# Streaming the key and value caches in 8 MB units through three slots, with the K transpose in place, instead of 4 MB units through five

## Chip, cores, metric

One core of one Trainium2 chip. The metric is the device time of one execution in microseconds. The kernel before takes 662.42 us (median of 4 runs, 661.61 to 662.64). Most differences here are well under 1%, so nearly all kernels are measured in five rounds, with each kernel run beside the kernel before on the same chip.

## The reference

One decode step: layer norm, attention of 16 query heads over 8 cached K/V heads of 32,768 tokens, output projection, then layer norm and a small feed-forward net with the mish activation.

```python
def _A_ref(x, k_cache, v_cache, wq, wo):        # x [1,1,448], caches [1,8,32768,256] bf16
    q = (x @ wq).reshape(B, Sq, 16, 256).transpose(0, 2, 1, 3)
    k = jnp.repeat(k_cache, 2, axis=1); v = jnp.repeat(v_cache, 2, axis=1)
    p = softmax(einsum("bhqd,bhkd->bhqk", q, k) * 256 ** -0.5)
    o = einsum("bhqk,bhkd->bhqd", p, v)
    return o.transpose(0, 2, 1, 3).reshape(B, Sq, 4096) @ wo
h  = x + _A_ref(layernorm(x), ...)
h2 = h + mish(layernorm(h) @ w1 + b1) @ w2      # w1 [448,1792], w2 [1792,448]
```

The two caches are 268 MB, nearly all the bytes that are read.

## The kernel before

A unit is TU = 64 tokens per partition: 128 x 64 tokens x 256 values of bf16, 4 MB, one DMA. Each partition reads one contiguous row of 64 x 512 B = 32 KB. Units go into a ring of five slots.

```python
TU = 64; CT = 16                       # tokens per partition in a unit, in a group
RING = 5 * TU * Dh * 2                 # bytes per partition

def pump():                            # issue loads, in order, as long as there is room
    while st["next"] < len(loads):
        key, nbytes, issue = loads[st["next"]]
        ...                            # next place in the ring
        if any(a < pos + nbytes and pos < b for a, b, _ in live):
            return
        ...
        tiles[key] = issue(pos)

def kv_issue(src, g, u, a, b):
    def issue(pos):
        t = region(pos, (b - a) * Dh).rearrange("p (t d) -> p t d", d=Dh)
        rows = src[0, g, u * UT:(u + 1) * UT, :].rearrange("(p t) d -> p t d", p=P)
        nc.sync.dma_start(out=t, in_=rows[:, a:b, :])
        return t
    return issue
```

K is transposed in blocks of 32 x 32 by VectorE (DVE) into one of three small tiles; the unit's slot is then free for the next load. TensorE (PE) does 8 matmuls for each group of 16 tokens.

```python
def transpose_next():                  # one group ahead of the matmuls
    nc.vector.transpose(out=kt_ring[n % 3][:]..., in_=tiles[key][:, t0:t0 + CT]...)
    if t0 + CT == key[3] - key[2]:
        done(key)                      # K slot free
```

K runs one head ahead of V (NU = 4 units). The softmax of a head is cut into small steps (`i0` to `i4`: VectorE, PE and ScalarE in turn) which `hook()` puts between the groups that follow. At the end, `wo` (the output projection, 3.7 MB) is loaded after the last K unit, ahead of the last four V units, and the projections of the first seven heads stand ahead of the third-last and second-last V unit. Behind the last V unit come w1 and w2.

Of the kernel before, what the change touches and what calls it, by code (L numbers as in the profile page):

```python
# [24 lines left out]
def kernel(  # L25
# [13 lines left out]
    nc = tc.nc  # L39
# [5 lines left out]
    F = B_w1.shape[1]  # L45
    assert Dh == 256 and Hq == 2 * G and G == 8 and HD == 4096 and D == 448
    CT = 16
    TU = 64
    UT = TU * P
    CPU_ = TU // CT  # L50
    NU = Sk // UT
# [12 lines left out]

    W = 160
    DQ = D // 4
    RING = 5 * TU * Dh * 2

    const = ctx.enter_context(tc.tile_pool(name="const", bufs=1))
    small = ctx.enter_context(tc.tile_pool(name="small", bufs=4))  # L70
    ps = ctx.enter_context(tc.tile_pool(name="ps", bufs=1, space=bass.MemoryType.PSUM))
    ps_m = ctx.enter_context(tc.tile_pool(name="ps_m", bufs=2, space=bass.MemoryType.PSUM))
    ctx.enter_context(tc.manual_schedule())
# [5 lines left out]

    loads = []  # L80
    live = []
    st = {"next": 0, "pos": 0}

    def plan(key, nbytes, issue):
        loads.append((key, nbytes, issue))

    tiles = {}

    def pump():
        while st["next"] < len(loads):  # L90
            key, nbytes, issue = loads[st["next"]]
            pos = st["pos"]
            for _ in range(2):
                if pos + nbytes > RING:
                    pos = 0
                for a, b, kk in live:
                    if kk[0] == "wo" and a < pos + nbytes and pos < b:
                        pos = b
            if any(a < pos + nbytes and pos < b for a, b, _ in live):
                return  # L100
            live.append((pos, pos + nbytes, key))
            tiles[key] = issue(pos)
            st["pos"] = pos + nbytes
            st["next"] += 1

    def done(key):
        live[:] = [x for x in live if x[2] != key]
        pump()
# [45 lines left out]
    NK = G * NU  # L154
    H = TU // 2
    kpieces = {k: [(0, TU)] for k in range(NK)}
    kpieces[0] = [(0, H), (H, TU)]
    vpieces = {v: [(0, TU)] for v in range(NK)}
    vpieces[NK - 2] = [(0, H), (H, TU)]
    vpieces[NK - 1] = [(0, H), (H, H + 16), (H + 16, H + 24), (H + 24, TU)]  # L160
    order = []
    for k in range(NK + NU):
        if k < NK:
            order += [("k", k, a, b) for a, b in kpieces[k]]
        if k >= NU:
            order += [("v", k - NU, a, b) for a, b in vpieces[k - NU]]
        if k == NK - 1:
            order.append(("wo",))
    for kt in range(KTD):
        plan(("wq", kt), HD * 2 if kt < 3 else HD, wq_issue(kt))  # L170
    for key in order:
        if key[0] == "wo":
            plan(key, Hq * 2 * D * 2, wo_issue)
        else:
            g, u = divmod(key[1], NU)
            plan(key, (key[3] - key[2]) * Dh * 2,
                 kv_issue(A_k_cache if key[0] == "k" else A_v_cache, g, u, key[2], key[3]))
    plan(("w1", 0), 7 * F, w1_issue)
    plan(("w2", 0), FT * D * 2, w2_issue)

    xr_bf = const.tile([1, D], BF16)
    nc.scalar.dma_start(out=xr_bf[:], in_=A_x[0])
    b1r = big[0:1, RING // 2 - F:RING // 2]
    nc.scalar.dma_start(out=b1r, in_=B_b1.rearrange("(o f) -> o f", o=1))
    pump()

# [19 lines left out]
    maskT = const.tile([P, KTD], F32)  # L206
    nc.vector.memset(maskT[:], 1.0)
    nc.vector.memset(maskT[0:64, 3:4], 0.0)
    par = const.tile([1, 2, P], F32)
    nc.vector.memset(par[:], 0.0)  # L210
    for hh in range(2):
        nc.vector.memset(par[:, hh].rearrange("o (k e) -> o k e", e=2)[:, :, hh:hh + 1], -1.0)  # L212
    maskpar = const.tile([P, 2], F32)
    nc.vector.tensor_reduce(out=maskpar[:], in_=ident_f[:].rearrange("p (k e) -> p e k", e=2), axis=AX.X, op=ALU.add)  # L214
    hb2 = const.tile([P, KTD, 2], BF16)
# [11 lines left out]
    nc.vector.memset(oT_ps[:], 0.0)  # L227
    nc.vector.memset(hT_ps[:], 0.0)

    kt_ring = [const.tile([P, CT, Dh], BF16, name=f"kt{i}") for i in range(3)]  # L230
    p_ring = [const.tile([P, CT * 32], BF16, name=f"p{i}") for i in range(2)]
    pt_ring = [const.tile([P, CT, 32], BF16, name=f"pt{i}") for i in range(2)]
    rden = const.tile([P, G, 2], F32)
    og = const.tile([P, G, 2, 2], BF16)
# [6 lines left out]
    nc.gpsimd.tensor_scalar(out=vpe[:], in0=mv[:, 1:2], scalar1=EPS, scalar2=None, op0=ALU.add)  # L241
    rstd = small.tile([1, 1], F32, tag="ln_rstd")
    nc.gpsimd.tensor_tensor(out=rstd[:], in0=vpe[:], in1=negh[0:1], op=ALU.pow)  # L243
    xn_bf = const.tile([1, D], BF16)
    nc.vector.tensor_scalar(out=xn_bf[:], in0=xr_bf[:], scalar1=mv[:, 0:1], scalar2=rstd[:, 0:1],
                            op0=ALU.subtract, op1=ALU.mult)
    xeo = const.tile([1, 2, P], BF16)
    nc.vector.memset(xeo[:], 0.0)
    for e in range(2):
        nc.vector.tensor_copy(out=xeo[:, e].rearrange("o (r e) -> o r e", e=2)[:, :, e], in_=xn_bf[:, 3 * P:D])  # L250
# [30 lines left out]
    qrow_ps = ps_m.tile([NCH, P], BF16, tag="m")  # L281
    nc.tensor.transpose(out=qrow_ps[:], in_=qT_sb[:], identity=ident_bf[:])

    chunks = [(("k", k, a, b), k * CPU_ + t // CT, t - a) for k in range(NK) for a, b in kpieces[k] for t in range(a, b, CT)]
    tr = {"n": 0}

    def transpose_next():
        n = tr["n"]
        if n >= len(chunks):
            return  # L290
        key, _, t0 = chunks[n]
        tr["n"] += 1
        nc.vector.transpose(out=kt_ring[n % 3][:].rearrange("p t d -> p (t d)").bitcast(F32),  # L293
                            in_=tiles[key][:, t0:t0 + CT].rearrange("p t d -> p (t d)").bitcast(F32))
        if t0 + CT == key[3] - key[2]:
            done(key)

    Qin = const.tile([P, P], BF16)
    for i in range(4):
# [13 lines left out]
            nc.vector.tensor_copy(out=dst, in_=src)  # L313

    weights(0)
    transpose_next()

    def x_of(j, e):
        jhi, jl = j // 2, j % 2
# [10 lines left out]

    def k_chunk(n):
        g, c = divmod(n, NCK)
        transpose_next()
        if c == NCK // 2 and g + 1 < G:
            weights(g + 1)
        ktv = kt_ring[n % 3][:].rearrange("p t (j b e) -> p t j b e", j=4, b=32, e=2)
        s = s_ring[g % 2]
        for i in range(8):
            j, e = i // 2, i % 2
            nc.tensor.matmul(s[:], lhsT=QW[g % 2][:, x_of(j, e), 30 - 2 * c:30 - 2 * c + P], rhs=ktv[:, :, j, :, e],  # L340
                             start=(c == 0 and i == 0), stop=(c == NCK - 1 and i == 7))
        if c == NCK - 1:
            softmax(g)

    def softmax(g):
        s = s_ring[g % 2]
        p_ = p_ring[g % 2]
        pt = pt_ring[g % 2]
        m = small.tile([P, 1], F32, tag="m1", name=f"m1_{g}")
        mT = ps_m.tile([1, P], F32, tag="m", name=f"mT_{g}")  # L350
        m2 = small.tile([1, 2], F32, tag="m2", name=f"m2_{g}")
        nm_ps = ps_m.tile([P, 1], F32, tag="m", name=f"nm_{g}")
        nm = small.tile([P, 1], F32, tag="nm", name=f"nms_{g}")
        L = small.tile([P, 1], F32, tag="L", name=f"L_{g}")
        Lm = small.tile([P, 2], F32, tag="Lm", name=f"Lm_{g}")
        den = ps_m.tile([P, 2], F32, tag="m", name=f"den_{g}")

        def i0():
            nc.vector.reduce_max(out=m[:], in_=s[:], axis=AX.X)  # L359
            nc.tensor.transpose(out=mT[:], in_=m[:], identity=ident_f[:])  # L360

        def i1():
            nc.vector.reduce_max(out=m2[:], in_=mT[:].rearrange("o (k e) -> o e k", e=2), axis=AX.X)  # L363
            for hh in range(2):
                nc.tensor.matmul(nm_ps[:], lhsT=par[:, hh], rhs=m2[:, hh:hh + 1], start=(hh == 0), stop=(hh == 1))  # L365

        def i2():
            nc.vector.tensor_copy(out=nm[:], in_=nm_ps[:])  # L368
            nc.scalar.activation(out=p_[:], in_=s[:], func=ACT.Exp, bias=nm[:], scale=1.0, accum_out=L[:])  # L369

        def i3():
            ready.add(g)
            nc.vector.transpose(out=pt[:].rearrange("p t c -> p (t c)"), in_=p_[:])  # L373
            nc.vector.tensor_scalar(out=Lm[:], in0=maskpar[:], scalar1=L[:, 0:1], scalar2=None, op0=ALU.mult)

        def i4():
            nc.tensor.matmul(den[:], lhsT=ones_f[:], rhs=Lm[:], start=True, stop=True)  # L377
            nc.vector.reciprocal(out=rden[:, g], in_=den[:])  # L378
        pending.extend([lambda: None, i0, i1, i2, i3, i4])

    def v_chunk(g, c, vn, t0):
        assert g in ready
        pt = pt_ring[g % 2]
        o = o_ring[g % 2]
        last = NCK - 1 if g < G - 1 else NCK - 1 - CPU_
        for t2 in range(CT // 2):
            nc.tensor.matmul(o[:], lhsT=pt[:].rearrange("p t c -> p (t c)")[:, 64 * t2 + 2 * c:64 * t2 + 2 * c + 34],  # L387
                             rhs=vn[:, t0 + 2 * t2:t0 + 2 * t2 + 2, :].rearrange("p t d -> p (t d)"),
# [7 lines left out]

    def evac(g):
        o = o_ring[g % 2]
        osb = small.tile([34, 512], F32, tag="osb", bufs=2, name=f"osb_{g}")

        def e0():
            nc.scalar.copy(out=osb[:], in_=o[:])  # L402
# [29 lines left out]
    for key in order:  # L432
# [4 lines left out]
        if kind == "k":  # L437
            for t in range(a, b, CT):
                k_chunk(nk)
                nk += 1  # L440
                hook()
            continue
        if i == NK - 3:
            for gg in range(4 if a == 0 else 0):
                project(gg)
        if i == NK - 2 and a == 0:
            for gg in range(4, G - 1):
                project(gg)
        if i < NK - 1:
            for t in range(a, b, CT):  # L450
                v_chunk(g, u * CPU_ + t // CT, tiles[key], t - a)
                hook()
        else:
            for t in range(a, b, min(CT, b - a)):
                n = min(CT, b - a)
                v_cols(u * CPU_ + t // CT, t % CT, tiles[key][:, t - a:t - a + n], n)
            if pending:
                hook()
        done(key)
    og_copy(G - 1)  # L460
    project(G - 1)
# [108 lines left out]
```

## Time and profile before

| | before |
|---|---|
| time | 662.42 us |
| moved | 279.4 MB, 423 GB/s over the span |
| share of the 16 DMA engines filled by the SyncE queue's packets | 98.9% |
| PE, DVE busy | 78%, 48% |
| one 32 KB packet | 1218 ns (median and mean of 7,808) |
| first engine's landing to the next unit's | 9.713 us for 4 MB, 432 GB/s |

These are lines of the profile's page of the kernel before. The second gives busy time by engine; the DMA row is the mean busy share of the 16 DMA engines in 40 equal slices, in tenths; then packets and the load queue with its share. The last is the costliest group: line, engine, operation, count, then busy us and mean ns, then the engine's idle time before it.

```profile
span 659.8 us, 5982 instructions
PE 516.9 (78%) x2673; PEld 228.1 (35%) x2673; DVE 315.3 (48%) x263; ACT 13.8 (2%) x30; POOL 3.1 (0%) x12
...
DMA  9999999999999999999999999999999999999996
...
DMA packets 14293, 279.37 MB, mean 423 GB/s; under 512 B 1338, under 2 KB 4539, under 8 KB 5308
...
q1 hardware_dynamic: 14264, 278.99, 98.9%
...
L293 DVE STREAM_TRANSPOSE kt<-big 128x2048 f32<-128x2048 f32 x128 | 288.0, 2289 | 217.6 <-DMA big<-in_A_k_cache_dram 191.1
```

The DMA row is full from the first slice to the last but one, while the transposes sit idle for 191 us waiting for K. Loads set the time. Only two things can then shorten it: making the bytes cost less, or making the ends shorter, where the queue has not begun or is already empty.

The end is the second reading. This is PE's timeline of the kernel before: start and length in us, then line, operation, tile and count; in brackets PE's idle time before it and who ended it. The last V unit's direct matmuls are line 427, w1's are L483, w2's L535.

```profile
606.82 0.38 PE L387 MATMUL o<-big,pt 128*34 128x512 bf16 x1
618.53 3.34 PE L387 MATMUL o<-big,pt 128*34 128x512 bf16 x8 [11.34 <-DMA big<-in_A_v_cache_dram]
...
638.51 7.08 PE L387 MATMUL o<-big,pt 128*34 128x512 bf16 x32
645.52 1.75 PE L427 MATMUL oT_ps<-pt,big 128*128 128x2 bf16 x64
...
648.24 1.83 PE L427 MATMUL oT_ps<-pt,big 128*128 128x2 bf16 x64
650.32 0.57 PE L421 MATMUL hT_ps<-og,big 128*128 128x1 bf16 x16 [0.25 <-DVE og L394]
651.14 0.51 PE L483 MATMUL h_ps<-hb,big 128*128 128x2 bf16 x14 [0.26 <-DVE hb L466]
...
655.38 1.48 PE L535 MATMUL y_ps<-big,actT 128*1 128x112 bf16 x56 [1.66 <-DVE actT L520]
```

PE stands idle for 11.3 us while `wo` is loaded ahead of V, and then has no more gap until 650: it is behind its data. The last V piece landed at 647.98 us (all 16 of its completions counted in the trace) and PE finished it only at 650.07.

### The profile page before, as it was taken

To read this page: it belongs to the slowest core of one execution; us is meant where nothing else is said; L and a number is where in the kernel's file an instruction comes from. 1 tells how busy PE (TensorE), PEld (TensorE's weight loads), DVE (VectorE), ACT (ScalarE), POOL (GpSimd) and SP (SyncE) were. 2 spreads that over 40 slices of the span, in tenths; PEclk is the share of its full clock that TensorE was granted. 3 is DMA by queue.
4 is the path that set the end of the run, shared out by engine and by line. 5 is a ranking of instruction groups with operands and counts; after the bars stand their busy time and mean duration, and the time that the engine had idled before them with its cause. 6 is when DMAs were issued, how large, how long until landed. Compare 5 with 4: busy or idle time off the path is not lost.

```text
span 659.8 us, 5982 instructions
## 1 busy us (share of the span) xinstructions
PE 516.9 (78%) x2673; PEld 228.1 (35%) x2673; DVE 315.3 (48%) x263; ACT 13.8 (2%) x30; POOL 3.1 (0%) x12
## 2 busy tenths in 40 slices
PE   3577389949986699748997399974999669978596
PEld 2223134314432244313443144421443224333255
DVE  3599455528345366434654254552744447533001
ACT  1000000000000000000000000000000000000000
POOL 1000000000000000000000000000000000000000
PEclk9989889969998599986999789995999879999696
DMA  9999999999999999999999999999999999999996
GB/s 365 429 444 436 421 438 421 442 421 436 435 422 445 417 440 427 430 433 425 441 421 439 429 430 435 424 435 432 433 428 431 427 436 436 424 433 398 431 414 231
DMA packets 14293, 279.37 MB, mean 423 GB/s; under 512 B 1338, under 2 KB 4539, under 8 KB 5308
## 3 DMA queue, kind: packets, MB, share of 16 engines
q1 hardware_dynamic: 14264, 278.99, 98.9%
q8 instruction: 21, 0.34, 0.2%
q14 instruction: 4, 0.03, 0.0%
q10 hardware_dynamic: 4, 0.00, 0.0%
HBM read 278.99 MB, written 0.00 MB: 423 GB/s over the span
## 4 chain that ended last, share of the span: by engine, by line
issue 98%; DVE 1%; PE 0%; POOL 0%; POOLq 0%; ACT 0%
PE y_ps L535 0%; POOLq L565 0%; DVE stt L237 0%; POOL rstd L243 0%; DVE maskpar L214 0%; DVE par L210 0%; DVE res L538 0%; DVE hq L218 0%; DVE z L506 0%; DVE dn L517 0%; ACT e__3117 L509 0%; POOL vpe L241 0%; DVE dn L516 0%; DVE e L512 0%; DVE par L212 0%
## 5 line engine op out<-in xcount | busy, mean ns | idle before, releaser
L293 DVE STREAM_TRANSPOSE kt<-big 128x2048 f32<-128x2048 f32 x128 | 288.0, 2289 | 217.6 <-DMA big<-in_A_k_cache_dram 191.1
L340 PE MATMUL s<-kt,qw 128*128 128x512 bf16 x1024 | 243.3, 387 | 48.7 <-DVE kt L293 48.6
L387 PE MATMUL o<-big,pt 128*34 128x512 bf16 x992 | 244.3, 406 | 21.9 <-DMA big<-in_A_v_cache_dram 11.3
L340 PEld LDWEIGHTS <-qw 128*128 128x128 bf16 x1024 | 98.0, 98 | 186.5 <-issue 79.0
L387 PEld LDWEIGHTS <-pt 128*34 128x34 bf16 x992 | 98.3, 103 | 155.5 <-issue 48.9
L360 PE MATMUL mT<-ident_f,m 128*1 128x128 f32 x8 | 2.8, 347 | 58.7 <-DVE m L359 58.7
L360 PEld LDWEIGHTS mT<-ident_f,m 128*1 128x1 f32 x8 | 0.6, 79 | 62.6 <-DVE m L359 62.1
L378 DVE RECIPROCAL rden<-den 128x2 f32<-128x2 f32 x8 | 1.4, 171 | 37.7 <-PE den L377 37.7
L369 ACT ACTIVATE p<-s,nms 128x512 bf16<-128x512 f32 x8 | 5.5, 688 | 556.5 <-DVE nms L368 556.5
L394 DVE TENSOR_TENSOR og<-oT_ps,rden 128x4 bf16<-128x4 f32 x8 | 1.3, 163 | 32.5 <-PE oT_ps L427 23.1
L368 DVE COPY nms<-nm 128x1 f32<-128x1 f32 x8 | 1.2, 152 | 26.5 <-PE nm L365 26.5
L408 PEld LDWEIGHTS oT_ps<-ident_f,osb 34*128 34x128 f32 x64 | 8.1, 193 | 3.0 <-issue 3.0
L408 PE MATMUL oT_ps<-ident_f,osb 34*128 34x2 f32 x64 | 8.8, 256 | 0.0
L373 DVE STREAM_TRANSPOSE pt<-p 128x512 bf16<-128x512 bf16 x8 | 5.7, 706 | 6.3 <-ACT p L369 6.3
L365 PEld LDWEIGHTS nm<-m,par 1*128 1x128 f32 x32 | 6.0, 262 | 6.2 <-issue 6.2
L365 PE MATMUL nm<-m,par 1*128 1x1 f32 x32 | 6.7, 309 | 0.5 <-DVE m L363 0.5
L359 DVE TENSOR_REDUCE m<-s 128x1 f32<-128x512 f32 x8 | 5.3, 657 | 2.3 <-PE s L340 2.3
L276 PE MATMUL qT_ps<-xnT,big 128*128 128x1 bf16 x128 | 4.0, 165 | 2.6 <-DMA big<-in_A_wq_dram 2.2
L402 ACT COPY osb<-o 34x512 f32<-34x512 f32 x8 | 4.6, 580 | 64.2 <-PE o L387 64.2
L313 DVE COPY qw<-QX 32x16 bf16<-32x16 bf16 x32 | 5.0, 157 | 0.4
L276 PEld LDWEIGHTS <-big 128*128 128x128 bf16 x128 | 3.7, 104 | 2.9 <-DMA big<-in_A_wq_dram 2.4
L363 DVE TENSOR_REDUCE m<-mT 1x2 f32<-1x128 f32 x8 | 2.2, 273 | 4.1 <-PE mT L360 4.1
(90 smaller groups left out, 48.9 us busy)
## 6 DMA issues: line engine op xcount, KB each, us to landing
big<-in_A_k_cache_dram SPq DMA_DIRECT2D x31, 4096.0 KB, 30.3
big<-in_A_v_cache_dram SPq DMA_DIRECT2D x30, 4096.0 KB, 39.2
big<-in_A_v_cache_dram SPq DMA_DIRECT2D x3, 2048.0 KB, 35.0
big<-in_A_k_cache_dram SPq DMA_DIRECT2D x2, 2048.0 KB, 17.4
big<-in_A_wo_dram SPq DMA_DIRECT2D x1, 3584.0 KB, 38.8
big<-in_A_wq_dram SPq DMA_DIRECT2D x3, 1024.0 KB, 6.9
big<-in_B_w_dram SPq DMA_DIRECT2D x4, 448.0 KB, 23.4
big<-in_A_v_cache_dram SPq DMA_DIRECT2D x1, 1024.0 KB, 39.9
```

What stands on the lines that cost most here:

```text
L276: nc.tensor.matmul(qT_ps[:, y:y + 1], lhsT=wt[:, cc * P:(cc + 1) * P], rhs=xnT[:, kx:kx + 1], start=False, stop=False, skip_group_check=True)
L293: nc.vector.transpose(out=kt_ring[n % 3][:].rearrange("p t d -> p (t d)").bitcast(F32), in_=tiles[key][:, t0:t0 + CT].rearrange("p t d -> ...
L313: nc.vector.tensor_copy(out=dst, in_=src)
L340: nc.tensor.matmul(s[:], lhsT=QW[g % 2][:, x_of(j, e), 30 - 2 * c:30 - 2 * c + P], rhs=ktv[:, :, j, :, e], start=(c == 0 and i == 0), stop ...
L359: nc.vector.reduce_max(out=m[:], in_=s[:], axis=AX.X)
L360: nc.tensor.transpose(out=mT[:], in_=m[:], identity=ident_f[:])
L365: nc.tensor.matmul(nm_ps[:], lhsT=par[:, hh], rhs=m2[:, hh:hh + 1], start=(hh == 0), stop=(hh == 1))
L369: nc.scalar.activation(out=p_[:], in_=s[:], func=ACT.Exp, bias=nm[:], scale=1.0, accum_out=L[:])
L373: nc.vector.transpose(out=pt[:].rearrange("p t c -> p (t c)"), in_=p_[:])
L387: nc.tensor.matmul(o[:], lhsT=pt[:].rearrange("p t c -> p (t c)")[:, 64 * t2 + 2 * c:64 * t2 + 2 * c + 34], rhs=vn[:, t0 + 2 * t2:t0 + 2 * ...
L402: nc.scalar.copy(out=osb[:], in_=o[:])
L408: nc.tensor.matmul(oT_ps[:, g, dh, :], lhsT=osb[:, tt * 256 + dh:tt * 256 + 255 + dh:2], rhs=ident_f[0:34, 32 * tt:32 * tt + 2], start=Fal ...
```

## The change

Its intent: fewer and longer transfers. A unit holds 128 tokens per partition, 8 MB, with 64 KB rows; there is room for three. To make that room K is transposed in its own slot, so that the slot stays taken until the last matmul has read it. The end is also rearranged: `wo` is loaded just before the last V unit, into the slot of the third-last one, and all seven early projections stand at the last V unit.

```diff
-    TU = 64
+    TU = 128
-    RING = 5 * TU * Dh * 2
+    UB = TU * Dh * 2
+    RING = 3 * UB
 ...
     for i, (kind, n) in enumerate(units):
+        if i == len(units) - 1:
             order.append(("wo",))
+            plan(order[-1], (i - 2) % 3 * UB, Hq * 2 * D * 2, wo_issue)
 ...
+            plan(order[-1], i % 3 * UB + a * Dh * 2, (b - a) * Dh * 2, kv_issue(src, g, u, a, b))
 ...
-        nc.vector.transpose(out=kt_ring[n % 3][:].rearrange("p t d -> p (t d)").bitcast(F32),
-                            in_=tiles[key][:, t0:t0 + CT].rearrange("p t d -> p (t d)").bitcast(F32))
-        if t0 + CT == key[3] - key[2]:
-            done(key)
+            kf = kv_flat(tr["n"]).bitcast(F32)
+            nc.vector.transpose(out=kf, in_=kf)
 ...
-        if i == NK - 3:
-            for gg in range(4 if a == 0 else 0):
-                project(gg)
-        if i == NK - 2 and a == 0:
-            for gg in range(4, G - 1):
-                project(gg)
+            if i == NK - 1 and a == 0:
+                for gg in range(G - 1):
+                    project(gg)
```

Cut: small tiles moved into the ring's free space, smaller pools, and the pieces in which the first K and last V unit are loaded (their sizes at the end are as before).

More of the change, by code (lines that the diff above doesn't have):

```diff
@@ L66 @@
     DQ = D // 4
-    RING = 5 * TU * Dh * 2
+    UB = TU * Dh * 2
+    RING = 3 * UB
     const = ctx.enter_context(tc.tile_pool(name="const", bufs=1))
-    small = ctx.enter_context(tc.tile_pool(name="small", bufs=4))
+    small = ctx.enter_context(tc.tile_pool(name="small", bufs=2))
     ps = ctx.enter_context(tc.tile_pool(name="ps", bufs=1, space=bass.MemoryType.PSUM))
@@ L81, with plan @@
     live = []
-    st = {"next": 0, "pos": 0}
-    def plan(key, nbytes, issue):
-        loads.append((key, nbytes, issue))
+    st = {"next": 0}
+    def plan(key, pos, nbytes, issue):
+        loads.append((key, pos, nbytes, issue))
     tiles = {}
@@ L90, in pump @@
         while st["next"] < len(loads):
-            key, nbytes, issue = loads[st["next"]]
-            pos = st["pos"]
-            for _ in range(2):
-                if pos + nbytes > RING:
-                    pos = 0
-                for a, b, kk in live:
-                    if kk[0] == "wo" and a < pos + nbytes and pos < b:
-                        pos = b
+            key, pos, nbytes, issue = loads[st["next"]]
             if any(a < pos + nbytes and pos < b for a, b, _ in live):
@@ L102, in pump @@
             tiles[key] = issue(pos)
-            st["pos"] = pos + nbytes
             st["next"] += 1
@@ L156 @@
     kpieces = {k: [(0, TU)] for k in range(NK)}
-    kpieces[0] = [(0, H), (H, TU)]
+    kpieces[0] = [(0, 32), (32, H), (H, TU)]
     vpieces = {v: [(0, TU)] for v in range(NK)}
     vpieces[NK - 2] = [(0, H), (H, TU)]
-    vpieces[NK - 1] = [(0, H), (H, H + 16), (H + 16, H + 24), (H + 24, TU)]
-    order = []
-    for k in range(NK + NU):
-        if k < NK:
-            order += [("k", k, a, b) for a, b in kpieces[k]]
-        if k >= NU:
-            order += [("v", k - NU, a, b) for a, b in vpieces[k - NU]]
-        if k == NK - 1:
-            order.append(("wo",))
@@ L169 @@
-    for kt in range(KTD):
-        plan(("wq", kt), HD * 2 if kt < 3 else HD, wq_issue(kt))
-    for key in order:
-        if key[0] == "wo":
-            plan(key, Hq * 2 * D * 2, wo_issue)
-        else:
-            g, u = divmod(key[1], NU)
-            plan(key, (key[3] - key[2]) * Dh * 2,
-                 kv_issue(A_k_cache if key[0] == "k" else A_v_cache, g, u, key[2], key[3]))
-    plan(("w1", 0), 7 * F, w1_issue)
-    plan(("w2", 0), FT * D * 2, w2_issue)
-    xr_bf = const.tile([1, D], BF16)
+    vpieces[NK - 1] = [(0, 32), (32, H), (H, H + 32), (H + 32, H + 48), (H + 48, H + 56), (H + 56, TU)]
@@ new lines @@
+    units = []
+    for k in range(NK + NU):
+        units += [("k", k)] if k < NK else []
+        units += [("v", k - NU)] if k >= NU else []
+    order = []
+    for kt in range(KTD):
+        plan(("wq", kt), 2 * UB + kt * HD * 2, HD * 2 if kt < 3 else HD, wq_issue(kt))
+    for i, (kind, n) in enumerate(units):
+        if i == len(units) - 1:
+            order.append(("wo",))
+            plan(order[-1], (i - 2) % 3 * UB, Hq * 2 * D * 2, wo_issue)
+        src, pieces = (A_k_cache, kpieces) if kind == "k" else (A_v_cache, vpieces)
+        g, u = divmod(n, NU)
+        for a, b in pieces[n]:
+            order.append((kind, n, a, b))
+            plan(order[-1], i % 3 * UB + a * Dh * 2, (b - a) * Dh * 2, kv_issue(src, g, u, a, b))
@@ L182, with scratch @@
+    plan(("w1", 0), (len(units) - 3) % 3 * UB + Hq * 2 * D * 2, 7 * F, w1_issue)
+    plan(("w2", 0), (len(units) - 2) % 3 * UB, FT * D * 2, w2_issue)
+    top = {"pos": RING // 2}
+    def scratch(np_, n):
+        top["pos"] -= n
+        return big[0:np_, top["pos"]:top["pos"] + n]
+    xr_bf = scratch(1, D)
     nc.scalar.dma_start(out=xr_bf[:], in_=A_x[0])
-    b1r = big[0:1, RING // 2 - F:RING // 2]
+    b1r = scratch(1, F)
     nc.scalar.dma_start(out=b1r, in_=B_b1.rearrange("(o f) -> o f", o=1))
@@ L208 @@
     nc.vector.memset(maskT[0:64, 3:4], 0.0)
-    par = const.tile([1, 2, P], F32)
+    par = const.tile([1, P + 2], F32)
     nc.vector.memset(par[:], 0.0)
-    for hh in range(2):
-        nc.vector.memset(par[:, hh].rearrange("o (k e) -> o k e", e=2)[:, :, hh:hh + 1], -1.0)
+    nc.vector.memset(par[:].rearrange("o (k e) -> o k e", e=2)[:, :, 0:1], -1.0)
     maskpar = const.tile([P, 2], F32)
@@ L228 @@
     nc.vector.memset(hT_ps[:], 0.0)
-    kt_ring = [const.tile([P, CT, Dh], BF16, name=f"kt{i}") for i in range(3)]
-    p_ring = [const.tile([P, CT * 32], BF16, name=f"p{i}") for i in range(2)]
+    p_ring = [const.tile([P, CT * 32], BF16, name=f"p{i}") for i in range(1)]
     pt_ring = [const.tile([P, CT, 32], BF16, name=f"pt{i}") for i in range(2)]
@@ L243 @@
     nc.gpsimd.tensor_tensor(out=rstd[:], in0=vpe[:], in1=negh[0:1], op=ALU.pow)
-    xn_bf = const.tile([1, D], BF16)
+    xn_bf = scratch(1, D)
     nc.vector.tensor_scalar(out=xn_bf[:], in0=xr_bf[:], scalar1=mv[:, 0:1], scalar2=rstd[:, 0:1],
                             op0=ALU.subtract, op1=ALU.mult)
-    xeo = const.tile([1, 2, P], BF16)
+    xeo = scratch(1, 2 * P).rearrange("o (e p) -> o e p", e=2)
     nc.vector.memset(xeo[:], 0.0)
@@ L282, with kv_flat, transpose_to @@
     nc.tensor.transpose(out=qrow_ps[:], in_=qT_sb[:], identity=ident_bf[:])
-    chunks = [(("k", k, a, b), k * CPU_ + t // CT, t - a) for k in range(NK) for a, b in kpieces[k] for t in range(a, b, CT)]
+    chunks = [(("k", k, a, b), t - a) for k in range(NK) for a, b in kpieces[k] for t in range(a, b, CT)]
     tr = {"n": 0}
-    def transpose_next():
-        n = tr["n"]
-        if n >= len(chunks):
-            return
-        key, _, t0 = chunks[n]
-        tr["n"] += 1
-        nc.vector.transpose(out=kt_ring[n % 3][:].rearrange("p t d -> p (t d)").bitcast(F32),
-                            in_=tiles[key][:, t0:t0 + CT].rearrange("p t d -> p (t d)").bitcast(F32))
-        if t0 + CT == key[3] - key[2]:
-            done(key)
+    def kv_flat(n):
+        key, t0 = chunks[n]
+        return tiles[key][:, t0:t0 + CT].rearrange("p t d -> p (t d)")
+    def transpose_to(n):
+        while tr["n"] <= n:
+            kf = kv_flat(tr["n"]).bitcast(F32)
+            nc.vector.transpose(out=kf, in_=kf)
+            tr["n"] += 1
     Qin = const.tile([P, P], BF16)
@@ L315 @@
     weights(0)
-    transpose_next()
     def x_of(j, e):
@@ L332, in k_chunk @@
         g, c = divmod(n, NCK)
-        transpose_next()
+        transpose_to(n + 1 if n + 1 < len(chunks) and chunks[n + 1][0] == chunks[n][0] else n)
         if c == NCK // 2 and g + 1 < G:
             weights(g + 1)
-        ktv = kt_ring[n % 3][:].rearrange("p t (j b e) -> p t j b e", j=4, b=32, e=2)
+        ktv = kv_flat(n).rearrange("p (t j b e) -> p t j b e", j=4, b=32, e=2)
         s = s_ring[g % 2]
@@ L346, in softmax @@
         s = s_ring[g % 2]
-        p_ = p_ring[g % 2]
+        p_ = p_ring[0]
         pt = pt_ring[g % 2]
@@ L364, in i1 @@
             for hh in range(2):
-                nc.tensor.matmul(nm_ps[:], lhsT=par[:, hh], rhs=m2[:, hh:hh + 1], start=(hh == 0), stop=(hh == 1))
+                nc.tensor.matmul(nm_ps[:], lhsT=par[:, hh:hh + P], rhs=m2[:, hh:hh + 1], start=(hh == 0), stop=(hh == 1))
         def i2():
@@ L384, in v_chunk @@
         o = o_ring[g % 2]
-        last = NCK - 1 if g < G - 1 else NCK - 1 - CPU_
+        last = NCK - 1 if g < G - 1 else NCK - 1 - CPU_ // 2
         for t2 in range(CT // 2):
@@ L398, in evac @@
         o = o_ring[g % 2]
-        osb = small.tile([34, 512], F32, tag="osb", bufs=2, name=f"osb_{g}")
+        osb = small.tile([34, 512], F32, tag="osb", bufs=1, name=f"osb_{g}")
         def e0():
@@ L441 @@
                 hook()
-            continue
-        if i == NK - 3:
-            for gg in range(4 if a == 0 else 0):
-                project(gg)
-        if i == NK - 2 and a == 0:
-            for gg in range(4, G - 1):
-                project(gg)
-        if i < NK - 1:
+        elif i < NK - 1 or b <= H:
+            if i == NK - 1 and a == 0:
+                for gg in range(G - 1):
+                    project(gg)
             for t in range(a, b, CT):
@@ L453 @@
         else:
-            for t in range(a, b, min(CT, b - a)):
-                n = min(CT, b - a)
+            n = min(CT, b - a)
+            for t in range(a, b, n):
                 v_cols(u * CPU_ + t // CT, t % CT, tiles[key][:, t - a:t - a + n], n)
-            if pending:
-                hook()
+            hook(2)
         done(key)
```

## The prediction

> **What bounds the kernel now.** The profile's page gives 279.4 MB over a span of 659.8 us, 423 GB/s, with the DMA row at 9 tenths in all slices but the last; the SyncE queue's packets fill 98.9% of 16 engines. PE is 78% busy, DVE 48%, and both wait for loads (waits view: DVE 191 us for K tiles). So loads bound it. In the packet records a 32 KB packet (one partition's row of a 4 MB unit) takes 1218 ns in the mean; successive units land 9.71 us apart, 432 GB/s; 8 KB packets take 309 ns. From 309 and 1213 ns (the quick tenth of the 32 KB ones) I estimate 0.0368 ns per byte plus about 8 ns per packet. The Trainium skill's "DMA: Bandwidth & Descriptors" (Where 436 GB/s comes from) puts the ceiling at 435.2 GB/s; the measured 432 agrees, so the middle is nearly at it.
>
> **What the change does.** K/V units go from 4 MB (five slots) to 8 MB (three slots), rows from 32 to 64 KB; K is transposed in place, so a K slot is released after its last matmul. Counts of transposes and matmuls stay.
>
> 1. Packets: about 3,900 fewer large ones. At 8 ns each over 16 engines this saves about 2.0 us, plus 0.3 us of completion packets (9 ns each). If a 64 KB row goes as two packets, the saving is nil.
> 2. Slots: an 8 MB unit takes 19.4 us to land, so a slot may stay occupied 39 us after landing. K needs 8 transposes of 2.25 us plus matmuls of 1.9 us, about 20.5 us. V needs 8 x 1.93, about 15.5 us, beginning 1 us after landing. Slack is near 18 us; I expect no starvation.
> 3. The tight spot is the end: the output projection's weights reuse the slot of the third-last unit and stand in the queue right behind the second-last. Counting from the last K unit's landing: K done at about 20, that V unit with softmax steps at 36.5, next unit landed at 38.8[...]. The queue just avoids running dry; a slower clock would cost 1 to 2 us. Part is hidden, since engines finish a unit 3 to 5 us apart near the end (landing records).
> 4. Tail: PE now ends the last V piece 2 us after it landed, because of a backlog; the last weight lands at 655.8 us and the span ends 4 us later. The new order leaves less backlog: about 0.5 us saved.
>
> **Sum.** 662.4 - 1.4 (2.3 for packets, at 60%) - 0.5 (tail) + 0.5 (possible gap): about 661. Faster by 2% would need nearly every byte at the ceiling.
>
> Predicted 660.9 us, range 658.3 to 663.8. Chances: faster by over 2% 0.01, within 2% 0.95, slower by over 2% 0.04.
>
> **What would show it.** Right: about 3,900 fewer packets, 64 KB ones at about 2,428 ns; units landing 19.4 us apart; DMA row at 9s; a transpose still near 2.25 us. Item 1 is wrong if packets stay 32 KB or 64 KB ones take over 2,436 ns; item 2 if the DMA row dips or landings spread; item 3 if a gap shows before the projection's weights.
>
> **What would make it wrong.** 64 KB-pitch rows read more slowly from HBM (the same page, Latency and other measured facts, reports slow-downs for power-of-two pitches from 512 KiB; nothing here shows it for 64 KiB), slower in-place transposes, or a slot wait I missed.

## The result

658.78 us (median of 9 runs, 658.63 to 658.93) against 662.42 us (13 runs, 661.45 to 662.73). The ratio is 0.9947, with a 95% interval of 0.9937 to 0.9956. Ratios are the mean time of one kernel's fast runs over that of the other's in the same rounds, so not quite the ratio of the medians. The gain is 3.6 us by the medians: inside the predicted range, 0.5 us above its lower end, and more than twice the 1.5 us that its central value stood for.

The same lines of the page, after:

```profile
span 657.1 us, 5846 instructions
PE 529.9 (81%) x2673; PEld 233.7 (36%) x2673; DVE 313.4 (48%) x262; ACT 13.8 (2%) x30; POOL 3.1 (0%) x12
...
DMA  9999999999999999999999999999999999999996
...
DMA packets 10116, 279.36 MB, mean 425 GB/s; under 512 B 874, under 2 KB 4075, under 8 KB 4844
...
q1 hardware_dynamic: 10088, 278.99, 98.9%
...
L290 DVE STREAM_TRANSPOSE big<-big 128x2048 f32<-128x2048 f32 x128 | 284.8, 2280 | 197.7 <-DMA big<-in_A_k_cache_dram 197.5
```

There are 4,177 packets fewer (464 of them 4-byte completion packets) and the same bytes. The queue is as full as before, at a slightly higher rate. The transpose in place takes 2280 ns, as into another tile. The packet records hold 3,712 packets of 64 KB, at 2424 ns in the mean: one 64 KB row is one packet.

The end, after, in PE's timeline (L421 the last V unit's direct matmuls, L472 w1, L524 w2):

```profile
630.58 9.78 PE L381 MATMUL o<-big,pt 128*34 128x512 bf16 x32 [1.46 <-DMA big<-in_A_v_cache_dram]
640.91 1.75 PE L421 MATMUL oT_ps<-pt,big 128*128 128x2 bf16 x64 [0.56 <-DMA big<-in_A_v_cache_dram]
...
645.99 0.59 PE L421 MATMUL oT_ps<-pt,big 128*128 128x2 bf16 x16 [0.40 <-DMA big<-in_A_v_cache_dram]
...
649.33 0.53 PE L472 MATMUL h_ps<-hb,big 128*128 128x2 bf16 x14 [0.34 <-DMA big<-in_B_w_dram]
...
653.85 0.36 PE L524 MATMUL y_ps<-big,actT 128*1 128x112 bf16 x8 [0.17 <-DMA big<-in_B_w_dram]
```

Now PE waits for data at each step and finishes the last V piece about 0.6 us after its landing (645.94). From the landing of the last weight to the end of the span, both read from the trace:

```
                 last weight landed   span ends   difference
before                 655.77           659.83       4.05
after                  653.80           657.14       3.34
```

So in these two traces 2.0 us come from an earlier last landing and 0.7 from a shorter end. (The profiled run of before, at 661.61 us, is one of its quickest, hence 2.7 and not 3.6.) Which part of the change brings each is a matter for experiments.

### The profile page after: what moved, and what is told of

It is laid out like the page before. It is cut to its first block, busy times and chain, and to the rows that moved or that the text cites. A ratio compares the mean times of both kernels' runs of the same rounds, so it can differ in the third digit from the quotient of the medians.

```text
span 657.1 us, 5846 instructions
## 1 busy us (share of the span) xinstructions
PE 529.9 (81%) x2673; PEld 233.7 (36%) x2673; DVE 313.4 (48%) x262; ACT 13.8 (2%) x30; POOL 3.1 (0%) x12
## 4 chain that ended last, share of the span: by engine, by line
DMA 57%; DVE 22%; PE 19%; SPq 1%; issue 0%; DVEq 0%
DMA big<-in_A_k_cache_dram 51%; DVE big L290 22%; PE o L381 15%; DMA big<-in_B_w_dram 5%; PE s L334 2%; SPq L107 1%; DMA big<-in_A_wq_dram 1%; DVE qw L308 1%; PE nm L359 1%; PE den L371 0%; PE mT L354 0%; PE oT_ps L402 0%; PE y_ps L524 0%; DVE res L527 0%; DVE og L388 0%
## 5 line engine op out<-in xcount | busy, mean ns | idle before, releaser
L290 DVE STREAM_TRANSPOSE big<-big 128x2048 f32<-128x2048 f32 x128 | 284.8, 2280 | 197.7 <-DMA big<-in_A_k_cache_dram 197.5
L334 PE MATMUL s<-big,qw 128*128 128x512 bf16 x1024 | 273.1, 419 | 110.0 <-DVE big L290 108.8
L381 PE MATMUL o<-big,pt 128*34 128x512 bf16 x992 | 223.3, 383 | 1.5 <-DMA big<-in_A_v_cache_dram 1.5
L334 PEld LDWEIGHTS <-qw 128*128 128x128 bf16 x1024 | 105.6, 104 | 271.1 <-issue 124.2
L381 PEld LDWEIGHTS <-pt 128*34 128x34 bf16 x992 | 94.8, 98 | 118.8 <-issue 11.0
L402 PEld LDWEIGHTS oT_ps<-ident_f,osb 34*128 34x128 f32 x64 | 11.1, 255 | 5.1 <-issue 5.1
L402 PE MATMUL oT_ps<-ident_f,osb 34*128 34x2 f32 x64 | 11.8, 303 | 0.0
L359 PEld LDWEIGHTS nm<-m,par 1*128 1x128 f32 x32 | 4.1, 185 | 3.9 <-issue 3.9
L359 PE MATMUL nm<-m,par 1*128 1x1 f32 x32 | 4.8, 249 | 0.5 <-DVE m L357 0.5
L421 PE MATMUL oT_ps<-pt,big 128*128 128x2 bf16 x128 | 3.8, 164 | 1.0 <-DMA big<-in_A_v_cache_dram 1.0
```

Source lines behind the costliest of these rows:

```text
L290: nc.vector.transpose(out=kf, in_=kf)
L334: nc.tensor.matmul(s[:], lhsT=QW[g % 2][:, x_of(j, e), 30 - 2 * c:30 - 2 * c + P], rhs=ktv[:, :, j, :, e], start=(c == 0 and i == 0), stop ...
L359: nc.tensor.matmul(nm_ps[:], lhsT=par[:, hh:hh + P], rhs=m2[:, hh:hh + 1], start=(hh == 0), stop=(hh == 1))
L381: nc.tensor.matmul(o[:], lhsT=pt[:].rearrange("p t c -> p (t c)")[:, 64 * t2 + 2 * c:64 * t2 + 2 * c + 34], rhs=vn[:, t0 + 2 * t2:t0 + 2 * ...
L402: nc.tensor.matmul(oT_ps[:, g, dh, :], lhsT=osb[:, tt * 256 + dh:tt * 256 + 255 + dh:2], rhs=ident_f[0:34, 32 * tt:32 * tt + 2], start=Fal ...
```

## The experiments

**Theory A:** most of the gain is packets; a packet has a fixed cost beside its bytes. The rest is the rearranged end. **Theory B:** the gain comes from the new slots, from fewer DMAs or from the end, and the packet size does nothing. A further question is whether the slack that I had reckoned for three slots is real. Four kernels ran, and the kernel before beside them took 662.16 us (9 runs, 661.56 to 662.98).

### 1. The changed kernel with 32 KB runs

The unit is two contiguous halves; each partition takes 64 tokens of each. The slots, the order and the number of DMAs stay.

```diff
-  rows = src[0, g, u * UT:(u + 1) * UT, :].rearrange("(p t) d -> p t d", p=P)
+  R = TU // 2
+  rows = src[0, g, u * UT:(u + 1) * UT, :].rearrange("(h p t) d -> p h t d", h=2, p=P)
```

> The changed kernel with one thing undone: the 8 MB unit is read as two contiguous 4 MB halves, so each partition's row comes in two runs of 32 KB; still one DMA per unit, same slots, same order, in-place transposes (the tokens are dealt to the partitions differently, for K and V alike, so the result is the same). Theory A (most of the gain is the packets: a 64 KB packet takes 2424 ns, two of 32 KB take 2436): about 3,700 packets more at 12.5 ns over 16 engines, +2.9 us, so about 661.7 us. Theory B (the gain comes from the new slots, fewer DMAs and the reordered tail): stays at 658.8 us.

Measured: 660.94 us (5 runs, 660.77 to 661.11), ratio to before 0.9982 (0.9968 to 0.9995). 2.2 us of the gain are gone and 1.2 us are left. Theory B falls, and A holds with a smaller size than its 2.9 us. (The rows lie side by side in memory, so their distance halves with their length; no run here separates the two.)

### 2. The changed kernel with 16 KB runs

As above with `TU // 4` and `h=4`.

> As the run before, with four runs of 16 KB per row. Theory A: a 16 KB packet took 612 to 615 ns in the traces, so four cost 24 to 36 ns more than one of 64 KB; over 3,700 rows and 16 engines that is +5.6 to +8.4 us on the changed kernel, 664.4 to 667.2 us. Theory B: no change, 658.8 us.

Measured: 665.52 us (665.41 to 665.63), ratio 1.005 (1.0038 to 1.0063): now slower than the kernel before, though it has the new slots, the in-place transpose and the new end. The size can be read more cleanly from the landing records. In the mean over 20 units in the middle, the first completions of two successive units are this far apart (in the changed kernel 19.340 to 19.367 us, so hardly anything has held up the engines that finish first):

```
run length   us per 8 MB unit (16 engines, 8 rows each)   per packet more
64 KB        19.351   (after)
32 KB        19.424   (experiment 1)                      73 ns / 8    =  9.1 ns
16 KB        19.575   (experiment 2)                     151.5 ns / 16 =  9.5 ns
```

The kernel before spaces its 4 MB units at 9.713 us, 19.426 for two, the same as experiment 1. Over these three lengths the cost is nearly one constant per packet, 9.1 to 9.5 ns. The recorded durations (2 x 1218 against 2424 ns) give 12 ns and overstate it: 8 packets in 19.351 us are 2419 ns each, less than the 2424 recorded, and with 32 KB it is 1214 against 1218, so the recorded times of successive packets overlap by a few ns. The Trainium skill's "DMA: Bandwidth & Descriptors", section Measured, states about 10.5 ns per packet, from the floor of a 4 KB load; the measured cost for large packets is a little below that.

### 3. 32 KB runs and two DMAs for each unit

Experiment 1, with all units loaded in two pieces, as many DMAs as before the change:

```diff
-    kpieces = {k: [(0, TU)] for k in range(NK)}
+    kpieces = {k: [(0, H), (H, TU)] for k in range(NK)}      # and the same for vpieces
```

> As the first run (32 KB runs), and each unit is loaded by two DMAs of 4 MB, as many as in the kernel before. Theory A: the same as the first run plus at most 0.3 us of completion packets, about 662.0 us. If the number of DMAs costs by itself (a pause between one and the next), it would be slower than the first run by more than 1 us: 29 more DMAs at some tens of ns each to 0.1 us.

Measured: 661.08 us (660.93 to 661.23), 0.14 us more than experiment 1, less than the spread of either's five runs (0.3 us). Beyond the 0.3 us that was allowed for completion packets, the number of DMAs costs nothing that shows.

### 4. The kernel before with the new end only

`wo` moves to the place before the last V unit, and the seven projections move with it. Nothing else is touched.

```diff
-        if k == NK - 1:
-            order.append(("wo",))
+        if k == NK + NU - 1:
+            order.append(("wo",))
 ...
-        if i == NK - 3: ... project(0..3)
-        if i == NK - 2 and a == 0: ... project(4..6)
+        if i == NK - 1 and a == 0: ... project(0..6)
```

> The kernel before, with only the end reordered as in the change: the output projection's weights are loaded just before the last V unit and all seven early projections stand before that unit's work. Theory A: the time from the last weight's landing to the end of the span falls from 4.06 to about 3.3 us, so 662.4 - 0.75, about 661.7 us. If the reordered end gave nothing, 662.4 us; if it gave most of the gain, 659 to 660 us.

Measured: 661.04 us (660.82 to 661.09), ratio 0.9982 (0.9969 to 0.9994): 1.1 us by the medians. In its trace the last weight lands at 655.95 and the span ends at 659.3, 3.36 us later, against 4.05 before. PE waits for its data again, here in experiment 4's timeline:

```profile
638.32 3.13 PE L421 MATMUL hT_ps<-og,big 128*128 128x1 bf16 x112 [5.15 <-DMA big<-in_A_wo_dram]
643.18 1.87 PE L427 MATMUL oT_ps<-pt,big 128*128 128x2 bf16 x64 [1.73 <-DMA big<-in_A_v_cache_dram]
...
646.77 2.04 PE L427 MATMUL oT_ps<-pt,big 128*128 128x2 bf16 x64
```

It finishes the last V piece 0.6 us after its landing (648.18), as in the changed kernel, and no longer 2.1 us after it: the backlog is gone.

Experiments 3 and 4 meet from both sides. The first has three slots, 8 MB units and the in-place transpose, the second five slots, 4 MB units and separate tiles. Both load the caches in 32 KB runs, mostly in DMAs of 4 MB, and have the new end: 661.08 and 661.04 us. In sum, the slots and the in-place transpose by themselves bring nothing that shows; they are what 64 KB rows cost in memory.

### 5 and 6. How much slack three slots leave

A transpose of a transpose gives the data back, so doing it three times is still right and adds VectorE work without new memory:

```diff
-            nc.vector.transpose(out=kf, in_=kf)
+            for _ in range(3 if tr["n"] % 4 == 0 else 1):     # % 2 in the second
+                nc.vector.transpose(out=kf, in_=kf)
```

> The changed kernel with more VectorE work in each K unit: every fourth group of 16 tokens is transposed three times in place instead of once (a transpose of a transpose gives the first data back, so the result is right). A K unit then needs 12 transposes, 4 x 2.25 = 9 us more, and leaves its slot about 29.5 us after it landed, of 39. Theory (slack near 18 us, loads alone set the time): unchanged, 658.8 us, within 0.5. Rival (three slots are only just enough): several us slower, since a late slot would delay each of 16 K units.

> As the run before with every second group transposed three times: 16 transposes per K unit, 18 us more, so K leaves its slot about 38.5 us after landing[...]. The theory says that here the queue begins to run dry: 5 to 30 us slower (0.5 to 2 us at each of some 15 K units). If it stays at 658.8, the slack is larger than reckoned; if the run before was slow already, it is smaller.

Measured, beside the kernel before at 662.39 us: 668.12 us (4 runs, 667.3 to 669.01), ratio 1.0094 (1.0078 to 1.0109), and 755.98 us (4 runs, 754.95 to 756.76). Both are slower than I expected. The windows view of the first (length, then busy us and counts of PE, PE weight loads, DVE, ACT and POOL; last the granted clock, the DMA share and GB/s):

```profile
60.00:108.00 48.00, 34.16 (x125) 13.60 (x124) 47.74 (x31) 0.78 (x2) 0.00 (x0) 0.84 0.97 418
108.00:115.00 7.00, 6.70 (x31) 2.83 (x30) 5.36 (x4) 0.00 (x0) 0.00 (x0) 1.00 0.66 236
...
130.00:600.00 470.00, 386.26 (x1634) 164.06 (x1632) 339.91 (x207) 8.13 (x18) 0.00 (x0) 0.92 1.00 431
600.00:652.00 52.00, 50.92 (x344) 24.35 (x344) 9.89 (x11) 1.84 (x4) 0.00 (x0) 0.93 0.98 400
```

From 130 to 600 us the queue is full: in the middle the slack is at least 9 us, as reckoned. The loss is at the two ends. The first three units are all K, with no V between them, and land 19.4 us apart while VectorE needs 27 us for each (12 transposes of 2.25): in the row from 60 to 108 us it is busy for 47.74 of 48. The sixth unit's load, waiting for the third K unit's slot, is issued at 110.61 us, and the DMA share falls to 0.66. In the changed kernel the same load is issued at 92.91 us, 15.3 us before the first engine has landed the unit ahead of it (108.21). At the other end the last K unit leaves PE later and the V units behind it pile up: the span ends 7.6 us after the last landing (657.98 to 665.6) instead of 3.3. Of the 8.5 us between the two profiled spans (665.6 and 657.1), 4.2 are the later landing and 4.3 the longer end.

The second shows what else I had missed. Its page has these two rows:

```profile
DMA  9999691999959999599959999599995999689796
GB/s 375 433 446 439 285 393 53 389 443 442 396 223 445 401 435 391 223 446 442 443 230 387 428 411 442 226 429 407 422 411 227 442 389 439 289 335 442 274 424 233
```

The queue runs dry again and again. Its timeline, between one K unit's transposes and the next's:

```profile
346.98 0.69 DVE L354 TENSOR_REDUCE m<-s 128x1 f32<-128x512 f32 x1 [3.92 <-PE s L335]
...
352.43 0.71 DVE L368 STREAM_TRANSPOSE pt<-p 128x512 bf16<-128x512 bf16 x1 [0.91 <-ACT p L364]
...
356.97 0.17 DVE L373 RECIPROCAL rden<-den 128x2 f32<-128x2 f32 x1 [3.72 <-PE den L372]
357.06 9.18 DVE L291 STREAM_TRANSPOSE big<-big 128x2048 f32<-128x2048 f32 x4
```

The next K unit's first transpose (357.06) follows straight on the reciprocal, with no idle time of its own: its data was there. VectorE works in program order, as this timeline shows, and the softmax steps in its queue wait for PE, which works on V groups in between. They hold VectorE for some 10 us, from 347 to 357, of which 2 are work, and before them it waits 3.9 us for PE to finish the K unit. Two K units of 16 transposes at 2.28 us are 73 us; with these 14 and about 1 more VectorE needs some 88 us for a head, where two K and two V units land in 77.4. The reciprocals, one for each head, show where the 97 us arise. The first head's stands at 120.9 us, 34.5 later than in the changed kernel (86.4): here the first K units follow each other without V, as in the run before. From the first to the eighth it is 588.7 us against 519.6, 69 more, or 9.9 a head, close to the 10 of this sum. The end gives some 7 back. In the changed kernel the hold falls into time in which VectorE would wait for K anyway (197.5 us in all, in the page's lines above).

### 7. The packet cost applied to w2

At 9.3 ns a packet, long runs should pay elsewhere too. The order of the hidden features is free, so one partition can take 7 rows of w2 side by side, if the columns of w1 are picked at a stride of 7 instead of 2.

```diff
-        off = base + (256 * (k // 2) + k % 2 if k < 6 else 768)
-        return slice(off, off + (2 * P - 1 if k < 6 else P), 2 if k < 6 else 1)
+        return slice(base + k, base + k + 7 * (P - 1) + 1, 7)
 ...
-            v = B_w2[e * F // 2:(e + 1) * F // 2, :]                                    # 5 DMAs, 1024 packets
+            v = B_w2[e * F // 2:(e + 1) * F // 2, :].rearrange("(p k) n -> p k n", k=7)  # 3 DMAs, 384 packets
```

> The packet cost applied elsewhere: the last weight (B_w2) is read in longer runs (7 hidden features per partition side by side, 384 packets instead of 1024; the columns of B_w1 are picked with a stride of 7 to match). At the 9.3 ns that one packet more was seen to cost (unit spacing of an engine 19.350, 19.423 and 19.575 us at 64, 32 and 16 KB), 640 packets over 16 engines are 0.37 us: about 658.4 us, if the wider stride of the B_w1 weight loads costs nothing. If those loads are slower, unchanged or worse.

Measured: 659.21 us (5 runs, 659.17 to 659.33), 0.4 us slower than the change. The last weight did land earlier, at 653.54 instead of 653.80 us. But the w1 weight loads became slower. This is the groups view over the last 18 us, of the changed kernel:

```profile
L472 PEld LDWEIGHTS <-big 128*128 128x128 bf16 x56 | 2.1, 108 | 0.8 <-DMA big<-in_B_w_dram 0.4 <-issue 0.3
```

and of this run:

```profile
L468 PEld LDWEIGHTS <-big 128*128 128x128 bf16 x56 | 3.4, 154 | 0.3 <-issue 0.3
```

108 ns became 154, and the last matmuls start at 653.02 instead of 652.39. The last matmuls no longer wait for w2: the end is now set by the compute chain. The Trainium skill's "SBUF — State Buffer", section Door 1, says that two hits per 16-byte line are needed for full bandwidth: a stride of 2 bf16 values gives four and a stride of 7 about one, and the two times agree with that. No run here tries strides in between.

### 8. The same with the query weights in 32 KB rows

Four rows of wq on each of 112 partitions, one DMA with 112 packets instead of four with 512; the input vector is split to match.

```diff
-                nc.sync.dma_start(out=t, in_=A_wq[kt * P:(kt + 1) * P, :])             # and the rest, 4 DMAs
+        nc.sync.dma_start(out=t, in_=A_wq.rearrange("(p r) c -> p r c", r=4))          # 112 partitions
```

> As the run before, and the query weights are read with four rows per partition on 112 partitions (112 packets of 32 KB instead of 512 of 4 and 8 KB, one DMA): 400 packets less, 0.23 us, so about 658.2 us, if the query, ready some 3 us later, is still ready when the first K piece is transposed (20 us); else the first K work starts later, which the slack should hide.

Measured: 664.86 us (664.43 to 665.14), 5.65 us more than experiment 7. The weights landed at 18.11 us instead of 11.93, and the page's rate in the first slice fell to 234 GB/s (368 in the changed kernel). In the packet records all 16 engines are busy from 4 to 16 us, but the 112 packets take 2,037 ns in the mean (1,486 to 2,767), while the other 384 of 32 KB take 1,218. The time is lost before the first K piece has landed (its first engine is done at 21.79 us instead of 16.19). Since the queue is full from then on, nothing later makes up for it: the last weight lands 5.7 us later than in experiment 7 (659.24 and 653.54). That the 112 partitions are at fault is likely, since this load alone has a new shape; but it also reads four rows as one, in a single DMA, and what slows the packets was not tested.

No version tried beats the change.

## Why the prediction was right

The range held (658.78 in 658.3 to 663.8) and the mechanism was right, but the central value was 2.1 us too high. Term by term:

1. **Packets.** Forecast: 2.3 us if a 64 KB row is one packet, entered at 60% as 1.4. It is one packet, at 2424 ns (forecast 2428). Measured: 2.2 us by experiment 1 (2.3 with the completion packets, by experiment 3), at 9.1 ns a packet where I had estimated 8. The mis-sized step is the factor of 60%: the full estimate was right.
2. **Slots.** "I expect no starvation" held. "Slack is near 18 us" did not: it was worked out for the middle of the kernel, and left out the three K units in a row at the start, the pile-up at the end, and VectorE's softmax steps, which wait for PE. 9 us more per K unit cost 9.3 us, at the two ends only, and 18 us more cost 97.
3. **The gap before the projection's weights.** Forecast: "just avoids running dry", entered as 0.5 us. Measured: none, and far from it: the first engine finishes these weights 9.62 us after the unit ahead of them, against 9.55 in the kernel before. In the changed kernel SyncE issues the load at 603.12 us, 8.3 us before the first engine finishes the unit ahead of it (611.43), though PE leaves the third-last V unit only at 611.28. The forecast let the load wait for the whole unit. But `wo` fills 28 KB of the 64 KB slot and waits only for the matmuls that read those bytes, the first 56 of 128 tokens, which PE works through from 595.93 to about 603 us. The issue in SyncE's timeline:

```profile
603.12 0.39 SPq L124 DMA_DIRECT2D big<-in_A_wo_dram  x1
```

   From an issue to its first packet the traces show about 1.0 us when the queue is empty (0.74 to 1.76 us in the kernel before, 94.60 to 95.56 in experiment 6). The gap that the forecast feared does open in experiment 5, where K leaves later: there the load is issued at 617.00 us, after the first engine has finished the unit ahead (616.15), and that engine finishes `wo` 12.2 us after that unit. The last engine does so after 10.0 us, against 9.6 in the changed kernel, so most of the gap is hidden by the spread of the engines, as the forecast said.

4. **The end.** Forecast 0.5 us; experiment 4 measured 1.1 (0.7 in the trace). The cause named, PE's backlog, is what the timelines show. Whether the later `wo` or the later projections remove it was not separated. The kernel before has two groups of times (below); against the quicker one beside experiment 4 (661.56 to 661.80) the gain is 0.7 us, as in the trace.

Together: 662.4 - 2.2 - 1.1 = 659.1, and 658.8 was measured; the remaining 0.3 us is within what the kernel before varies by. That variation stays open: its runs lie at 661.5 to 662.0 or at 662.3 to 663.0 us, while those of every kernel with the new end that was not slowed on purpose lie within 0.7 us; no trace of the slower kind of run was at hand to compare.

## What to carry to other kernels

When the load queue is full from end to end, compute cannot be traded for time. What is left is the fixed cost of each packet (here 9 ns, 0.3% of the time between 32 and 64 KB rows, 0.7% between 16 and 32 KB) and the few microseconds after the last landing, and each should be sized on its own. Slack for a slot must be reckoned at the start and the end too, and through every queue that works in program order: extra work that the middle hid completely cost 9.3 us at the ends. And a longer run is only free if the reader of the data does not pay for it: the w2 rows landed 0.26 us earlier and the kernel still became 0.4 us slower, with w1's weight loads at 154 ns instead of 108.

## What the Trainium skill lacked or had wrong

- "DMA: Bandwidth & Descriptors": it has a measured per-packet cost for small packets only (about 10.5 ns, SWDGE). These runs add 9.1 to 9.5 ns for packets of 16 to 64 KB on the SyncE queue.
- The same page asks for a multiple of 16 as the outer dimension, ideally the 128 partitions, so that all 16 engines work. On 112 partitions they did all work here, but a 32 KB packet took 2,037 ns instead of 1,218, and the load landed at 18.11 us where 128-partition loads of the same bytes had landed at 11.93. The page has no such loss; its cause is open.
- The same page lists large power-of-two row pitches, from 512 KiB on, that slow DMA copies down. It has no word on 64 KiB, where this kernel saw no loss: 19.351 us per 8 MB is 433.5 GB/s, against its ceiling of 435.2.
- "Runtime: NRT & Kernel Launch", section Instruction fetch mechanics, calls the fetch of a 16 KiB instruction block mostly hidden. Here 21 such packets (0.34 MB) share the engines with the loads. The 64 KB packet next to one took 2.9 us instead of 2.42, and by the last V piece the 16 engines finish 5.1 us apart (640.80 to 645.94 us in the changed kernel). That the fetches cause most of this spread is likely but was not tested, and the page has no figure for it.
- "SBUF — State Buffer" has the 16-byte line rule without a figure for TensorE weight loads: 108 ns at a stride of 2 bf16 values, 154 ns at a stride of 7.
